# Attention and mixture of experts on one core: queries, keys and values laid out in DRAM by attention steps

## The chip, the core and the metric

The kernel runs on one of the eight cores of a Trainium2 chip. A core has a matrix engine (TensorE, PE in the rows; its weight loads are PEld), VectorE (DVE), ScalarE (ACT), GpSimd (POOL) and SyncE (SP), which here only issues transfers. Sixteen DMA engines move data between DRAM and on-chip memory, which has 128 partitions. The metric is the device time of one execution in microseconds (us); lower is better. Inputs are laid out on the host before the launch, outside of the time.

## What is computed

Attention over 8 batches, 8 heads, 576 positions, with 64 numbers per head. Half of the heads see a window of the last 32 positions, the other half every fourth of the last 128. The result, 4608 rows of 512, goes through a mixture of experts: each row picks one of 4 groups and one of its 4 experts, and is multiplied by that expert's two matrices.

```python
scores = scale * np.matmul(q, k.transpose(0, 1, 3, 2))
mask_plain = (rel >= 0) & (rel < window)
mask_dil = (rel >= 0) & (rel < window * dilation) & (rel % dilation == 0)
...
attn = np.exp(scores)
attn = attn / (np.sum(attn, axis=-1, keepdims=True) + 1e-09)
return np.matmul(attn, v).astype(np.float32)
...
h = np.maximum(xg[mask_e] @ w1[g, e], 0.0)
ye = h @ w2[g, e]
out[tok_idx] = combined[:, None] * ye
```

## The kernel before

Attention comes first, until about 150 us, and the experts after it. Attention is a loop over 36 steps (`for s in range(NT + 3)`, L944). A step takes 64 positions of a pair of batches, for all heads; it is software-pipelined: in turn `s` the loop issues the scores of step `s` (`scores`, L272), the transposes of step `s-1` (L302), the products with the values of step `s-2` (`av`, L314), and turns the finished rows of step `s-3` (L392). The order of PE and DVE is written out by hand, and that of SP and ACT too.

Three steps are a group `g`; there are 12 groups. Queries, keys and values are loaded by groups, by these functions:

- `load_q` (L109, its transfer L110) fills `qb`, 128 partitions of 3 x 512 numbers, 2 KB for each step. There are three such buffers; the third lies in space that later holds weights and is called `wa` in the rows.
- `load_k` (L112, L114) fills `kb` in two halves (`w` = 0 and 1), each of 64 partitions, every other one, with 1536 numbers. There are two such buffers, so the load of group `g+2` waits until the scores of group `g` are done. The first 256 columns are carried over from the group before (`carry_k`, L116).
- `load_v` (L122, L125) fills `vt` in two halves of 64 partitions with 3 x 520 numbers, 2,080 bytes for each step. There are three buffers; the third is also called `wa` in the rows. GpSimd makes a shifted copy, `vs` (`shift_v`, L127).

All of these loads go out on SP, in program order, with the stores of finished rows (`store_x`, L345, L350, L357, in runs of 1 KB) between them, and, late in the loop, with the first weights of the experts (`load_weights`, L641, runs of 4 KB). SP's transfers share eight semaphores (DMAHW0 to DMAHW7 below), so each transfer waits until the one eight places before it has landed.

At the start (L139 to L163) the loads of groups 0 to 2 are issued in one piece; of group 0, the queries of step 0 come alone, and then those of steps 1 and 2; the values likewise. In the loop, `load_k` of group `g+2` goes out at steps `s % 3 == 2` (first half) and the next `s % 3 == 0` (second half), `load_q` at `s % 3 == 0` and `load_v` at `s % 3 == 1`. For the last group, queries are loaded step by step and values in two cuts (L956, L976).

The function `layout` (L1183) lays the inputs out on the host. Queries of a group (`qa`) are [128, 3, 512], so a partition's three steps are one run of 6 KB in DRAM. Keys (`ka`) are [2, 64, 1536], and values (`va`) [128, 3, 8, 65]: 6,144 and 6,240 bytes a run.

Of the kernel before, what the change touches and what calls it, by code (L numbers as in the profile page):

```python
# [17 lines left out]
P = 128  # L18
# [37 lines left out]
def moe_attention_kernel(ctx, tc, q, k, k0, v, cmask, wgate, wpack, out):  # L56
    nc = tc.nc
# [34 lines left out]
    NQ, NK, NPT = 3, 2, 2  # L92
# [3 lines left out]
    qb = [qp.tile([P, 3, 512], F32, name=f"qb{i}") for i in range(NQ - 1)]  # L96
    qb.append(wa32[0][:, 2048 : 2048 + 3 * 512].rearrange("p (j n) -> p j n", j=3))
    VW = 2 * 3 * 8 * 65
    vt = [qp.tile([P, 2, 3, 8, 65], F32, name=f"vt{i}") for i in range(2)]
    vt.append(wa32[1][:, 0:VW].rearrange("p (w j s c) -> p w j s c", w=2, j=3, s=8))  # L100
    vs = [qp.tile([P, 2, 3, 8, 65], F32, name=f"vs{i}") for i in range(2)]
    kb = [qp.tile([P, 2, KW], F32, name=f"kb{i}") for i in range(NK)]
    pt = [qp.tile([P, 4, P], F32, name=f"pt{i}") for i in range(NPT)]
    st, dd, oo = {}, {}, {}
    three = lambda g: g % 3 if g < NG - 1 else 0
# [1 line left out]
    k0t = wa32[0][:, 0 : 2 * (8 * 96 + 32)].rearrange("p (w c) -> p w c", w=2)  # L107

    def load_q(g, j0=0, j1=3):  # L109
        nc.sync.dma_start(qb[three(g)][:, j0:j1], q[g, :, j0:j1])  # L110

    def load_k(g, halves=(0, 1)):  # L112
        for w in halves:
            nc.sync.dma_start(kb[g % NK][w:P:2, w, 256:], k[g, w])  # L114

    def carry_k(g):  # L116
        if g % 3 == 0:
# [4 lines left out]
    def load_v(g, cuts=(0, 3)):  # L122
        for j0, j1 in zip(cuts, cuts[1:]):
            for r in range(2):
                nc.sync.dma_start(vt[three(g)][r:P:2, r, j0:j1], v[g, 64 * r : 64 * r + 64, j0:j1])  # L125

    def shift_v(g, j0=0, j1=3):  # L127
        to, own, last = vs[g % 2], vt[three(g)], vt[three(g - 1)]
# [10 lines left out]
    first = ExitStack()  # L139
    first.enter_context(tc.manual_schedule(engines={mybir.EngineType.SP, mybir.EngineType.Activation}))  # L140
    load_q(0, 0, 1)
    nc.scalar.dma_start(masks[:, 0:2], cm[:, 0:2])
    nc.scalar.activation(warm, id32[:, 0:1], AF.Exp)
# [10 lines left out]
    for w in range(2):  # L154
        nc.sync.dma_start(k0t[w:P:2, w, 0 : 8 * 96], k0[w])
    load_q(0, 1, 3)
    load_k(0)
    load_v(0, (0, 1, 3))
    nc.gpsimd.dma_start(masks[:, 2:], cm[:, 2:])
    load_k(1)  # L160
    load_q(1)
    load_q(2)
    load_v(1)  # L163

    ones = cp.tile([P, P], BF16, name="ones")
# [778 lines left out]
    for s in range(NT + 3):  # L944
# [3 lines left out]
        if s % 3 == 2 and s // 3 + 2 < NT // 3:  # L948
            load_k(s // 3 + 2, (0,))
# [12 lines left out]
        if start:  # L962
            n = start[0]
# [10 lines left out]
        if s % 3 == 1 and 2 <= s // 3 + 2 < NG - 1:  # L974
            load_v(s // 3 + 2)
# [4 lines left out]
        if start:  # L980
            n = start.pop()
# [201 lines left out]
def layout(q, k, v, moe_w_group, moe_w_expert, moe_w1, moe_w2):  # L1183
    import numpy as np

    def seqs(a):
        a = np.asarray(a)
        d = a[:, 4:].reshape(B, 4, CLS, 4, D).transpose(0, 1, 3, 2, 4).reshape(B, 4, S, D)
        return np.stack([a[:, :4], d], axis=1).reshape(NBP, 2, 2, 2, 2, S, D)

    qs, ks, vs = seqs(q), seqs(k), seqs(v)
    qa = qs.reshape(NBP, 2, 2, 2, 2, 3, 3, 2, 32, D)
    qa = qa.transpose(0, 5, 9, 4, 6, 1, 2, 3, 7, 8).reshape(12, P, 3, 512)
    kpad = np.concatenate([np.zeros_like(ks[..., :32, :]), ks], axis=-2).reshape(*ks.shape[:5], 19, 32, D)
    blocks = lambda b: kpad[..., b, :, :].reshape(*ks.shape[:5], len(b) * 32, D)
    kg = [blocks([6 * i + b for b in (2, 4, 6, 1, 3, 5)]).reshape(*ks.shape[:5], 6, 32, D) for i in range(3)]
    ka = np.stack([a.transpose(0, 4, 7, 5, 1, 2, 3, 6) for a in kg], axis=1).reshape(12, 2, 64, 6 * 256)
    k0 = blocks([0, 2, 1])[0].transpose(3, 5, 0, 1, 2, 4).reshape(2, 64, 8 * 96)
    vw = vs.reshape(NBP, 2, 2, 2, 2, 3, 3, 2, 32, D)[..., ::-1, :, :]
    va = vw.transpose(0, 5, 4, 7, 8, 6, 1, 2, 3, 9).reshape(12, P, 3, 8, D)  # L1200
    va = np.concatenate([va, np.full_like(va[..., :1], 1.0 / SX)], axis=-1)

    cmask = np.full((2, 2, 32, len(MASKS), 2, 64), -1e9, np.float32)
    for mi, J in enumerate(MASKS):
        for a in range(2):
            for qq in range(32):
                i = 64 * J + 32 * a + qq
                for kd in range(2):
                    start = 0 if kd == 0 else (i // CLS) * CLS
                    for kk in range(64):  # L1210
                        half = (1 - a) * (kk // 32 - 1) - a * (kk // 32)
                        j = i - qq + 32 * half + kk % 32
                        if 0 <= i - j < 32 and j >= start:
                            cmask[:, a, qq, mi, kd, kk] = 0.0
    cmask = cmask.reshape(P, -1).astype(mybir.dt.np(BF16))
    wg = np.concatenate([np.asarray(moe_w_group), np.asarray(moe_w_expert).transpose(1, 0, 2).reshape(DM, 16)], axis=1)
    wg = np.concatenate([wg, np.zeros((DM, 12), wg.dtype)], axis=1)
    wgate = wg.reshape(4, P, 32).transpose(1, 0, 2).reshape(P, -1)
    w1 = np.asarray(moe_w1).reshape(NE, 4, P, FF).transpose(0, 2, 1, 3).reshape(NE, P, 4 * FF)
    w2 = np.asarray(moe_w2).reshape(NE, 8, P, DM).transpose(0, 2, 1, 3).reshape(NE, P, 8 * DM)  # L1220
    wpack = np.concatenate([w1, w2], axis=2).reshape(NE * P, 8192)
    c = np.ascontiguousarray
    return dict(q=c(qa), k=c(ka), k0=c(k0), v=c(va), cmask=c(cmask), wgate=c(wgate), wpack=c(wpack))
# [21 lines left out]
```

## Time and profile before

| | |
|---|---|
| median of 3 runs | 564.97 us (563.19 to 570.15) |
| the profiled execution's own time | 562.74 us |
| its span, from the first to the last instruction | 561.0 us |
| busy share of the span | PE 95%, PEld 69%, DVE 66%, ACT 57%, POOL 40% |
| packets of the queue that SP issues on (q1) | 72258, 113.65 MB, 65.7% of the 16 DMA engines |
| chain that ended last, by engine | PE 82%, DMA 6%, DVE 5%, issue 2%, ACT 2%, SP 2% |

The chain is followed back from the last instruction, at each step to what released it. A busy PE is not PE at its peak, because matmuls are pipelined and their ends are modelled. The packets of a queue take a share of 16 engines' time; a stretch of 1 us holds 16 us of engine time. "Landing" is the time from a transfer's issue to its semaphore.

### The profile page before, as it was taken

The numbers are of one execution on the slowest core, as the hardware profiler recorded it, in microseconds if no ns is written. First come the engines' busy times: TensorE is split into PE (matmuls) and PEld (weight loads), VectorE is DVE, ScalarE is ACT, GpSimd is POOL, SyncE is SP. The second block draws the span as 40 slices with busy tenths as digits, with TensorE's granted clock in tenths as the row PEclk, the third lists the DMA queues.
The fourth block names the chain that finished last, engine by engine and source line by source line (L and its number), as shares of the span: only waits on it lengthen the run. The fifth ranks groups of instructions, "written<-read, shape, count | busy, mean of one in ns | idle before, by whom it ended". The sixth has DMA issues, their size and how long they took to land.

```text
span 561.0 us, 16459 instructions
## 1 busy us (share of the span) xinstructions
PE 535.4 (95%) x6577; PEld 385.9 (69%) x6577; DVE 370.7 (66%) x846; ACT 317.1 (57%) x563; POOL 223.2 (40%) x211
## 2 busy tenths in 40 slices
PE   6899989997798999999999999999999999999995
PEld 3688878776676676556666666675766756787893
DVE  8776876876777336473868596757657667658650
ACT  6565546575555236464646564656656747647741
POOL 6796665758731423302231614133251421221212
PEclk9999999998999999999999999999999999999999
DMA  8988998798393726958697778779798798897731
GB/s 286 395 285 278 331 275 282 231 315 275 103 316 107 252 68 167 295 162 230 193 292 187 261 193 276 181 249 280 233 302 230 251 327 218 287 327 238 264 103 31
DMA packets 79265, 134.31 MB, mean 239 GB/s; under 512 B 42988, under 2 KB 52630, under 8 KB 79186
## 3 DMA queue, kind: packets, MB, share of 16 engines
q1 hardware_dynamic: 72258, 113.65, 65.7%
q0 software_dynamic: 6784, 19.51, 10.6%
q8 instruction: 53, 0.87, 0.6%
q14 instruction: 26, 0.21, 0.1%
q10 hardware_dynamic: 144, 0.07, 0.0%
HBM read 106.16 MB, written 19.29 MB: 224 GB/s over the span
## 4 chain that ended last, share of the span: by engine, by line
PE 82%; DMA 6%; DVE 5%; issue 2%; ACT 2%; SPq 2%; POOLq 0%; ACTq 0%; DVEq 0%
PE a L748 32%; PE y L841 26%; PE o L314 4%; PE y L859 4%; PE s L272 4%; DMA qb<-q 4%; PE yt L876 3%; PE t L302 3%; DMA kb<-k 2%; PE tx L392 2%; SPq L357 1%; PE lt_ps L417 1%; PE s L253 1%; DMA w<-wpack 1%; DVE wb2l L659 1%
## 5 line engine op out<-in xcount | busy, mean ns | idle before, releaser
L812 POOL DMA_INDIRECT out<-yr,sent x31 | 34.4, 1109 | 220.3 <-ACT yr L811 204.0
L756 DVE SCALAR_TENSOR_TENSOR hl<-a,hh 128x256 f16<-128x256 f32 (+13 forms) x144 | 61.1, 425 | 91.5 <-ACT hh L755 91.3
L748 PE MATMUL a<-xs,wb1h 128*128 128x256 f16 (+7 forms) x576 | 97.8, 275 | 2.5 <-DVE hl L756 2.5
L748 PE MATMUL a<-xs,wa 128*128 128x304 f16 (+7 forms) x864 | 96.6, 272 | 0.0
L755 ACT ACTIVATE hh<-a 128x256 f16<-128x256 f32 (+13 forms) x144 | 55.8, 388 | 63.0 <-PE a L748 62.2
L748 PEld LDWEIGHTS <-wa 128*128 128x128 f16 x864 | 79.2, 98 | 16.4 <-issue 0.2
L841 PEld LDWEIGHTS <-hh 128*128 128x128 f16 x480 | 46.9, 98 | 54.8 <-issue 1.2
L659 DVE SCALAR_TENSOR_TENSOR wa<-w,wa 128x1024 f16<-128x1024 f32 x58 | 69.5, 1217 | 19.1 <-ACT wa L662 19.1
L748 PE MATMUL a<-xs,wb1l 128*128 128x256 f16 (+7 forms) x288 | 78.3, 275 | 0.0
L841 PE MATMUL y<-wa,hh 128*128 128x512 f16 x240 | 73.9, 379 | 0.0
L662 ACT ACTIVATE wa<-w 128x1024 f16<-128x1024 f32 x64 | 66.8, 1055 | 1.5 <-DMA w<-wpack 1.3
L748 PEld LDWEIGHTS <-wb1h 128*128 128x128 f16 x576 | 55.1, 98 | 15.2 <-issue 3.0
L811 ACT ACTIVATE yr<-y,cs 128x512 f32<-128x512 f32 (+3 forms) x31 | 21.3, 687 | 64.4 <-issue 32.1
L687 POOL DMA_INDIRECT xr<-xd,sent x41 | 41.9, 1022 | 29.9 <-DVE sent L675 16.7
L659 DVE SCALAR_TENSOR_TENSOR wb2l<-w,wb2h 128x1024 f16<-128x1024 f32 x32 | 38.3, 1219 | 17.1 <-ACT wb2h L662 17.1
L303 ACT COPY pt<-t 128x512 f32<-128x512 f32 x36 | 21.1, 586 | 44.7 <-PE t L302 44.4
L841 PE MATMUL y<-wb2h,hh 128*128 128x512 f16 x120 | 45.6, 380 | 0.0
L841 PE MATMUL y<-wb2h,hl 128*128 128x512 f16 x120 | 45.5, 379 | 0.0
L841 PE MATMUL y<-wb2l,hh 128*128 128x512 f16 x120 | 45.5, 379 | 0.0
L841 PE MATMUL y<-wa,hl 128*128 128x512 f16 x120 | 45.5, 379 | 0.0
L314 PE MATMUL o<-vs,pt 128*32 128x130 f32 x576 | 40.4, 278 | 3.8 <-POOL wa L657 1.4
L282 DVE TENSOR_REDUCE mx<-s 128x8 f32<-128x512 f32 x36 | 24.6, 685 | 25.0 <-PE s L272 24.8
(206 smaller groups left out, 1073.1 us busy)
## 6 DMA issues: line engine op xcount, KB each, us to landing
w<-wpack SPq DMA_DIRECT2D x128, 512.0 KB, 5.1
kb<-k SPq DMA_DIRECT2D x24, 384.0 KB, 4.6
vt<-v SPq DMA_DIRECT2D x14, 390.0 KB, 7.1
qb<-q SPq DMA_DIRECT2D x7, 768.0 KB, 6.2
xd<-x SPq DMA_DIRECT2D x24, 192.0 KB, 5.8
wa<-v SPq DMA_DIRECT2D x6, 390.0 KB, 7.5
wa<-q SPq DMA_DIRECT2D x3, 768.0 KB, 8.6
xd<-x SPq DMA_DIRECT2D x32, 48.0 KB, 4.4
```

The source lines that it names most:

```text
L272: nc.tensor.matmul(s[32 * j : 32 * j + 32, c].rearrange("p w k -> p (w k)"), qv[:, (sl * 2 + a) * 32 : (sl * 2 + a) * 32 + 32], kv[:, :, f ...
L282: nc.vector.tensor_reduce(mx, s, axis=AX.X, op=ALU.max)
L314: nc.tensor.matmul(o[32 * j : 32 * j + 32, c // 2, at : at + 130], pt[n % NPT][:, c, 32 * j : 32 * j + 32], t[:, :, jl, bb * 4 + c, :], st ...
L659: nc.vector.scalar_tensor_tensor(l, w32, SW, h, ALU.mult, ALU.subtract)
L662: nc.scalar.mul(parts(i)[0], w32s[i], SW)
L687: nc.gpsimd.indirect_dma_start(out=xr[0:n], out_offset=None, in_=xd[0:known, :], in_offset=bass.IndirectOffsetOnAxis(ap=ent[0:n, t : t + 1 ...
L748: nc.tensor.matmul(a[:, 0:cap], ww[:, c * FF + f * P : c * FF + f * P + P], xx[:, c, 0:cap], start=(i == 0), stop=(i == len(mm) - 1),)
L755: nc.scalar.activation(hh[:, f, 0:cap], a[:, 0:cap], AF.Relu)
L756: nc.vector.scalar_tensor_tensor(hl[:, f, 0:cap], a[:, 0:cap], 0.0, hh[:, f, 0:cap], ALU.max, ALU.subtract)
L812: ins = nc.gpsimd.indirect_dma_start(out=out, out_offset=bass.IndirectOffsetOnAxis(ap=ent[0:n, t : t + 1], axis=0), in_=yr[0:n, :], in_off ...
L841: nc.tensor.matmul(yp, h[:, f, t * P : t * P + n], ww[:, f * DM : f * DM + DM], start=(i == 0), stop=(i == len(mm) - 1),)
L859: nc.tensor.matmul(yp[q * (P // g) : q * (P // g) + n, 0:wd], h[:, f, t * P : t * P + n], ww[:, f * DM + q * wd : f * DM + q * wd + wd], s ...
```

## The change

The arrays that the host hands over are transposed: queries of a group become [3, 128, 512], keys [2, 3, 64, 512], values [3, 128, 520]. Each step's part of a load is then one contiguous block. The load itself is a transfer of the same bytes to the same places, whose source has three runs of 2 KB (2,080 bytes for values) per partition where it had one of 6 KB. Loads of two steps of a group have two runs where they had one; loads of one step keep their run of 2 KB and lie closer together.

```diff
     def load_q(g, j0=0, j1=3):
-        nc.sync.dma_start(qb[three(g)][:, j0:j1], q[g, :, j0:j1])
+        nc.sync.dma_start(qb[three(g)][:, j0:j1], q[g, j0:j1].rearrange("j p n -> p j n"))
 
     def load_k(g, halves=(0, 1)):
         for w in halves:
-            nc.sync.dma_start(kb[g % NK][w:P:2, w, 256:], k[g, w])
+            to = kb[g % NK][w:P:2, w, 256:].rearrange("p (i n) -> p i n", i=3)
+            nc.sync.dma_start(to, k[g, w].rearrange("i p n -> p i n"))
...
             for r in range(2):
-                nc.sync.dma_start(vt[three(g)][r:P:2, r, j0:j1], v[g, 64 * r : 64 * r + 64, j0:j1])
+                to = vt[three(g)][r:P:2, r, j0:j1].rearrange("p j s c -> p j (s c)")
+                nc.sync.dma_start(to, v[g, j0:j1, 64 * r : 64 * r + 64].rearrange("j p n -> p j n"))
...
-    qa = qa.transpose(0, 5, 9, 4, 6, 1, 2, 3, 7, 8).reshape(12, P, 3, 512)
+    qa = qa.transpose(0, 5, 9, 4, 6, 1, 2, 3, 7, 8).reshape(12, P, 3, 512).transpose(0, 2, 1, 3)
...
-    ka = np.stack([a.transpose(0, 4, 7, 5, 1, 2, 3, 6) for a in kg], axis=1).reshape(12, 2, 64, 6 * 256)
+    ka = np.stack([a.transpose(0, 4, 7, 5, 1, 2, 3, 6) for a in kg], axis=1).reshape(12, 2, 64, 3, 512)
+    ka = ka.transpose(0, 1, 3, 2, 4)
...
+    va = va.reshape(12, P, 3, 520).transpose(0, 2, 1, 3)
```

The order of instructions is the same on every engine. What SP issues at the start, ahead of the loop, reads so before the change; a row is a transfer, target and source, its shape and the semaphores it waits for:

```order
L125 DMA vt_110<-v 64x1040 [waits DMAHW2_49]
L114 DMA kb_115<-k 64x1536 [waits DMAHW3_49,DVE_49]
L114 DMA kb_115<-k 64x1536 [waits DMAHW4_49,Activation_49]
L110 DMA qb_109<-q 128x1536 [waits DMAHW5_49]
L110 DMA wa_91<-q 128x1536 [waits DMAHW6_49]
L125 DMA vt_111<-v 64x1560 [waits DMAHW7_49,Activation_49]
```

and so after it, at the same place on SP:

```order
L127 DMA vt_110<-v 64x2x520 [waits DMAHW2_49]
L115 DMA kb_115<-k 64x3x512 [waits DMAHW3_49,DVE_49]
L115 DMA kb_115<-k 64x3x512 [waits DMAHW4_49,Activation_49]
L110 DMA qb_109<-q 128x3x512 [waits DMAHW5_49]
L110 DMA wa_91<-q 128x3x512 [waits DMAHW6_49]
L127 DMA vt_111<-v 64x3x520 [waits DMAHW7_49,Activation_49]
```

No row moved and no wait was added or removed; only the shapes differ, and the line numbers of what stands below `load_k`.

## Rows read from the trace of the kernel before

**Rows 1.** Busy time by engine in three stretches, granted clock, DMA share, GB/s

```profile
core 0: us, PE busy (x) PEld busy (x) DVE busy (x) ACT busy (x) POOL busy (x), PEclk, DMA share, GB/s
18.00:111.00 93.00, 90.50 (x2061) 74.95 (x2061) 69.38 (x180) 53.23 (x122) 65.71 (x58) 1.00 0.88 294
111.00:150.00 39.00, 33.29 (x689) 27.61 (x684) 27.51 (x83) 25.72 (x53) 27.76 (x21) 0.96 0.80 252
150.00:561.00 411.00, 400.83 (x3688) 276.82 (x3687) 259.67 (x529) 227.21 (x380) 117.15 (x110) 1.00 0.74 223
```

**Rows 2.** Waits from 18 to 150 us: who waited for what, us, times, longest

```profile
PE s L272 <- DMA kb<-k: 2.3, 1, 2.3
...
PE s L272 <- DMA qb<-q: 1.8, 1, 1.8
...
PEld s L272 <- DMA kb<-k: 0.3, 1, 0.3
```

**Rows 3.** PE's timeline: start, us, what, and the idle time before with its releaser

```profile
18.00 0.43 PE L272 MATMUL s<-kb,qb 128*32 128x128 f32 x8 [1.84 <-DMA qb<-q]
...
129.87 0.38 PE L272 MATMUL s<-kb,qb 128*32 128x128 f32 x5 [2.35 <-DMA kb<-k]
```

**Rows 4.** Busy time by engine in two short stretches, columns as in rows 1

```profile
130.40:133.80 3.40, 3.40 (x57) 3.01 (x49) 1.96 (x5) 0.00 (x0) 3.32 (x3) 0.50 0.95 339
134.00:140.00 6.00, 5.54 (x123) 4.48 (x121) 4.35 (x21) 5.07 (x12) 5.20 (x5) 1.00 0.92 283
```

**Rows 5.** The chain that ended last, in order: start us, us, what

```profile
3.63 6.60 DMA kb<-k
...
10.25 7.62 DMA qb<-q
...
53.07 0.51 SPq L114
...
53.62 5.34 DMA qb<-q
...
58.98 0.69 DVE x L370
...
126.32 3.42 DMA kb<-k
```

**Rows 6.** DMA issues: target, source, count, KB each, median us to landing

```profile
kb<-k SPq DMA_DIRECT2D x24, 384.0 KB, 4.6
vt<-v SPq DMA_DIRECT2D x14, 390.0 KB, 7.1
qb<-q SPq DMA_DIRECT2D x7, 768.0 KB, 6.2
...
wa<-v SPq DMA_DIRECT2D x6, 390.0 KB, 7.5
wa<-q SPq DMA_DIRECT2D x3, 768.0 KB, 8.6
...
vt<-v SPq DMA_DIRECT2D x4, 260.0 KB, 5.8
...
qb<-q SPq DMA_DIRECT2D x1, 512.0 KB
```

**Rows 7.** DMA queues, 12.5 to 15 us and then 1.8 to 3.0 us

```profile
DMA packets 201, 1.05 MB, mean 422 GB/s; under 512 B 29, under 2 KB 29, under 8 KB 201
...
q1 hardware_dynamic: 201, 1.05, 101.2%
...
q1 hardware_dynamic: 91, 0.19, 52.8%
q10 hardware_dynamic: 78, 0.04, 11.6%
```

**Rows 8.** Issues on SP: duration ns min/median/max, first and last start us

```profile
L114 SPq DMA_DIRECT2D kb<-k x24: 472/489/1259, 3.6 to 126.3; - x24
...
L110 SPq DMA_DIRECT2D qb<-q x12: 334/584/1047, 0.8 to 121.5; - x12
...
L345 SPq DMA_DIRECT2D xd<-x x24: 581/637/1487, 24.8 to 158.1; - x24
```

## The prediction

> **What bounds the kernel now.** I began with the three stretches by engine [rows 1]. From 18 to 111 us, the even part of the attention loop, TensorE (PE) is busy 90.50 of 93.00 us while the DMA engines are busy for 0.88 of the time. From 111 to 150 us PE is busy 33.29 of 39.00, at a mean granted clock of 0.96. From 150 us to the end PE is busy 400.83 of 411.00 us, and queries, keys and values are no longer loaded. So PE bounds the kernel nearly everywhere, and a change to these loads can act only where PE waits for one of them.
>
> The list of waits says where that is. After 18 us PE waited for a load of queries once, 1.8 us, and for a load of keys once, 2.3 us, and TensorE's weight load adds 0.3 [rows 2]. The PE timeline gives the places: the first score matmuls of group 1 start at 18.00 after 1.84 us of waiting for `qb<-q`, and those of group 11 (the last) at 129.87 after 2.35 us for `kb<-k` [rows 3]. The second wait costs more than itself: from 130.4 to 133.8 the granted clock is 0.50, that is 1.2 GHz of 2.4, and from 134 on it is 1.00 again [rows 4]. Before the clock fell the engine had done nothing for those 2.35 us. At half rate the 3.4 us did the work of 1.7, so 1.7 us were lost.
>
> The chain that ended last has DMA in the same places [rows 5]: `kb<-k` from 3.63 for 6.60 us and `qb<-q` from 10.25 for 7.62 us at the start, and `kb<-k` from 126.32 for 3.42. It also runs through SP's issues to `qb<-q` at 53.62 and from its landing to `DVE x` at 58.98. There it is nearly a tie, since PE itself is 97% busy in that stretch [rows 1].
>
> **What the change does.** No instruction moves and no byte is added: each load of queries, keys and values keeps its place on SP, its target and its semaphores. Only its runs are cut in three, because the steps of a group now lie apart in DRAM.
>
> How many more runs? A load of 768 KB for `qb` or `wa<-q` (7 + 3 of them) has 128 runs of 6 KB; each of 24 `kb` loads of 384 KB has 64; each of 14 + 6 value loads of 390 KB has 64 [rows 6]. That is 1,280 + 1,536 + 1,280 = 4,096 runs which become three, so 8,192 more. The one query load of 512 KB (128 runs) and the four value loads of 260 KB (64 each) go from one run to two: 384 more. Together **8,576 more runs**. Loads of a single step (256 KB, 130 KB) keep theirs.
>
> What does one more run cost? From 12.5 to 15 us the queues carry almost nothing but 6 KB runs: 201 packets, 29 of them small, 101.2% of 16 engines over 2.5 us [rows 7]. That is 40.48 us of engine time; less 29 small ones at some 10 ns (below), 40.2 / 172 = 234 ns a run. From 1.8 to 3.0 us the mask load on queue 10 shows 78 packets of 512 B and 11.6% of 16 x 1.2 us [rows 7], so 28.6 ns each. A line through both is 0.0365 ns a byte and **9.9 ns a packet**. A 2 KB run should then take 84.6 ns, three of them 254: 20 ns more than one of 6 KB. All of it: 8,576 x 9.9 / 16 = 5.3 us of the 16 engines' time, over 132 us of attention.
>
> The Trainium skill (DMA: Bandwidth & Descriptors, "Why small descriptors are slow") gives about 3 cycles a packet beside one per 32 bytes. By it, as an estimate, three packets instead of one are 6 cycles on 195, or 3.1%, 7 ns where the line gives 20; the whole would be 2.0 us of engine time instead of 5.3. The rows decide, and I keep 9.9 ns.
>
> **Issue.** SP's time for one issue, median, is 0.489 us for a key load (64 runs), 0.584 for a query load (128), and 0.637 for the store of L345, which has 64x3 runs [rows 8]. A key load will have the shape of that store, so I take 0.64, **+0.15 us**. For a query load of 384 runs I have bounds: 0.64 if the shape alone counts, and 1.27 if time goes with runs (0.637 / 192 x 384).
>
> **The sum, place by place.**
> *Start.* Before group 1's queries land, the engines work through what was issued ahead: one query load to two runs (128 more), both key halves of group 0 (256), values of group 0 (128), both key halves of group 1 (256) and these queries (256): 1,024 x 9.9 / 16 = **0.6 us**. The engines are full there [rows 7], so nothing hides it; PE would start at 18.6. Bounds: 0.2 (half of these runs moving while SP still issues) and 2.3, for a wait of 1.84 + 0.63 = 2.5 us is as long as the one after which the clock fell; the same 1.7 us could be lost here.
> *18 to 111 us.* PE waits for no load in this stretch, so the 768 runs more of a group, 768 x 9.9 / 16 = 0.5 us of engine time, are hidden by PE's work; if that cover were gone they would cost those 0.5 us a group. I take **0.3 us**, for two longer key issues (53.07 and the one before it) in the chain ahead of 53.62. Bounds 0 (the tie falls to PE) and 0.9 (two value issues at the same 0.15 and a query issue at 0.3 on the path too).
> *111 to 150 us.* Two key halves lie between 113.9 and 129.7: 256 x 9.9 / 16 = 0.16, and two issues, 0.30: **0.5 us** more in the wait of 2.35. Bounds 0 and 1.0 (the low clock lasting longer).
> *After 150 us.* Nothing of these loads is left: 0.
> Sum: **+1.4 us**. The profiled execution took 562.74 us (its span is 561.0), so 564.1. The median of the three runs shown is 564.97, which gives 566.4; between the two I forecast **565.3 us**.
>
> **Rivals.**
> *The DMA engines become the bound* (12%). Were attention paced by them, all 5.3 us would be on the path: 568 to 570 us. For it speaks their share of 0.88; against it, that PE is 97% busy in the same stretch and waits for none of them [rows 1, 2].
> *The clock falls at the start too* (13%). As above, +1.7: 566 to 568 us. It shows as a granted clock of 0.50 soon after 18 us.
> *Slower by over 2%: a 2 KB run costs far more than the line says* (8%). The kernel's very first load has 2 KB runs; queue 1 shows 91 packets and 52.8% of 16 x 1.2 us [rows 7], 111 ns each. At that price three runs are 333 ns, 99 more than now; 4,288 runs of 6 KB' worth of that, over 16, is 26.5 us of engine time. Attention leaves the engines idle for 132 - (0.88 x 93 + 0.80 x 39) = 19 us [rows 1], so at least 7.5 us would go on the path, and 512 x 99 / 16 = 3.2 at the start: 574 us, and up to 590 if the idle parts can't be filled because stores wait for compute. It decides from 19 x 16 / 4,288 = 71 ns per three runs, or 102 ns a run. Against it: that load ran into empty, just started queues, and the 512 B runs beside it took only 28.6 ns.
> The Trainium skill (Perfetto Trace Analysis, "DMA Optimizations") says that going from 2 KB to 4 or 8 KB can raise the throughput dramatically, which speaks against this change. It gives no price, and the steady 6 KB row and the 512 B row do not agree with a dramatic loss at 2 KB.
> *No cost, or a gain* (5%). If runs of 2 KB are stopped less by the stores between them, keys of group 11 could land earlier. The whole wait and its low clock are 2.35 + 1.7 = 4.0 us: 559 to 563 us. No row here shows a shorter run being held up less.
>
> **How the numbers follow.** The likeliest case (62%) covers 562 to 568 us with the spread of the runs shown. I let the range reach from 561.5 to 571: that takes in the first two rivals and most of the gain, and leaves out the slow rival and some of the tails. About 2% is 11 us here and is what can be told from no change. Only the slow rival exceeds it upward (0.08); for a gain over 2% there is too little waiting to be had (0.02); the rest, 0.90, is within.
>
> **What would show it.** Queue 1 should carry some 8,600 more packets. The first scores of group 1 should start near 18.6 us and those of group 11 wait some 2.8 us. A key issue should take 0.64 us. From 18 to 111 us PE should still be some 97% busy with no new wait for a load. I am wrong if PE waits for queries or keys in the middle of the loop, if steady 2 KB runs take over 100 ns, or if a clock of 0.50 shows in a new place.

## The result, and the profile after

The changed kernel takes **566.91 us** (median of 22 runs, 562.41 to 570.67). The kernel before, run beside it on the same chip, takes 564.0 (22 runs, 560.29 to 570.15). The ratio is **1.0054, with a 95% interval of 1.003 to 1.0078**: 3.0 us slower (1.7 to 4.4). The forecast was 565.3 us, in a range of 561.5 to 571.0, made of +1.4 us. So the time lies in the range and the change is within 2%, but the loss is about twice the sum, and the interval leaves +1.4 just outside.

The profiled execution of the changed kernel took 568.52 us with a span of 566.7. It stands 5.7 us above the span of before, more than the medians differ. The pair of traces therefore tells where time can go, not how much goes there on average. Line numbers below `load_k` are higher by one or two than before.

The three stretches, as in [rows 1]:

```profile
18.00:111.00 93.00, 89.07 (x1979) 73.62 (x1982) 68.09 (x175) 50.90 (x116) 61.55 (x54) 0.98 0.89 288
111.00:150.00 39.00, 31.06 (x672) 25.96 (x665) 26.81 (x80) 23.85 (x50) 29.25 (x22) 0.96 0.86 263
150.00:561.00 411.00, 405.94 (x3784) 281.00 (x3784) 262.52 (x535) 229.92 (x388) 120.44 (x111) 1.00 0.75 223
```

The last stretch is fuller only because the end moved from 561.0 to 566.7. In the first two, TensorE (PE) does less in the same time (matmuls 2061 to 1979, 689 to 672), and the DMA engines' share rises, most from 111 to 150 us: 0.80 to 0.86. The list of waits from 18 to 150 us says for what:

```profile
POOL vs L132 <- DMA vt<-v: 12.7, 5, 5.0
POOL vs L132 <- DMA wa<-v: 8.0, 2, 4.7
...
PE s L274 <- DMA kb<-k: 4.9, 3, 3.4
...
PEld s L274 <- DMA kb<-k: 2.6, 3, 1.6
...
PE s L274 <- DMA qb<-q: 1.8, 1, 1.8
```

PE and its weight load now wait for keys six times, 4.9 and 2.6 us, against 2.3 and 0.3 [rows 2]. The wait for queries is what it was. GpSimd's shifted copy `vs` waits 20.7 us for values, where the same two rows of before have 5.4 and 2.1.

Part of the keys' waiting is new in place. From 18 to 111 us alone the kernel before has one wait for keys, the 0.3 us of the weight load in [rows 2]. The changed kernel shows there:

```profile
PEld s L274 <- DMA kb<-k: 1.9, 2, 1.6
...
PE s L274 <- DMA kb<-k: 1.2, 1, 1.2
```

PE's timeline, to be laid beside [rows 3]: the transposes in turn 2, the first scores of group 1 (step 3) and of step 4, and the first scores of the last group (step 33):

```profile
15.27 0.66 PE L304 MATMUL t<-id,d 128*128 128x128 f32 x4 [0.63 <-ACT d L297]
...
17.92 1.55 PE L274 MATMUL s<-kb,qb 128*32 128x128 f32 x32 [1.78 <-DMA qb<-q]
...
22.67 0.54 PE L274 MATMUL s<-kb,qb 128*32 128x128 f32 x12
...
135.19 1.94 PE L274 MATMUL s<-kb,qb 128*32 128x128 f32 x32 [3.38 <-DMA kb<-k]
```

And two short windows behind those two waits, columns as in [rows 1] and [rows 4], with the first window of the kernel before as the third line:

```profile
18.20:21.70 3.50, 3.50 (x66) 3.11 (x56) 1.77 (x5) 0.00 (x0) 0.53 (x1) 0.53 1.05 386
134.40:137.90 3.50, 2.71 (x52) 2.74 (x56) 0.69 (x1) 0.00 (x0) 3.33 (x3) 0.51 1.03 373
...
18.20:21.70 3.50, 3.50 (x93) 2.98 (x89) 2.35 (x5) 1.05 (x3) 0.68 (x2) 1.00 1.05 416
```

The queries of group 1 land no later than before (scores at 17.92, before at 18.00). But the granted clock is 0.53 behind that wait, near 1.2 GHz of 2.4, where before it stayed at 1.00. Behind the last group's wait it is low in both kernels, and the wait itself has grown from 2.35 to 3.38 us.

With the start of each step's first score matmul in both traces, the 5.7 us can be laid out in order:

| stretch | before, us | after, us | difference |
|---|---|---|---|
| start to step 3 | 18.00 | 17.92 | -0.1 |
| steps 3 to 4 (clock 0.53) | 3.14 | 4.75 | +1.6 |
| steps 4 to 31 | 99.47 | 101.34 | +1.9 |
| steps 31 to 34 (last group) | 14.71 | 16.28 | +1.6 |
| step 34 to the end | 425.68 | 426.41 | +0.7 |

These are differences of two single executions. The traces of the experiments show how far the same stretches move by themselves. From step 4 to 31, two kernels whose loop loads are as before take 101.0 us (start3) and 103.7 (kf1), and four with runs of 2 KB take 100.6 to 102.1 (busy3, loop3, pad3, kf3). From step 34 on, where none of these loads is left, the same six take 426.6 to 432.9 us. So the pair alone doesn't show what the change costs in these stretches.

The DMA side shows what the change did to the transfers: queue 1 over the whole span, the same queue from 12.5 to 15 us, and the issues on SP, as in [rows 7] and [rows 8].

```profile
q1 hardware_dynamic: 80834, 113.65, 66.1%
```

```profile
DMA packets 515, 1.00 MB, mean 398 GB/s; under 512 B 29, under 2 KB 29, under 8 KB 515
...
q1 hardware_dynamic: 515, 1.00, 105.0%
```

```profile
L115 SPq DMA_DIRECT2D kb<-k x24: 602/612/2012, 3.6 to 129.5; - x24
...
L110 SPq DMA_DIRECT2D qb<-q x12: 372/593/1377, 0.8 to 126.2; - x12
```

80,834 less 72,258 is 8,576 packets. In the short window 105.0% of 16 x 2.5 us is 42.0 us; less 29 small ones at some 10 ns, 41.7 / 486 = **85.8 ns a run of 2 KB**, where 84.6 was forecast. The traces also have each packet by itself. From 0 to 150 us the median is 234 ns for 6,144 bytes (before), 84 for 2,048 (the change), 46 for 1,024 (all6) and 27 for 512 (q12). That is a straight line with 8 to 9 ns a packet on top of the bytes, and three runs of 2 KB take 18 ns more than one of 6 KB. A key issue takes 0.612 us and a query issue 0.593 in the median; four of those twelve query loads are of one step, and whole groups in the loop take 0.60 where before they took 0.58.

### The profile page after: what moved, and what is told of

Its sections match the earlier page's. It is cut to its first block, busy times and chain, and to the rows that moved or that the text cites. A ratio compares the mean times of both kernels' runs of the same rounds, so it can differ in the third digit from the quotient of the medians.

```text
span 566.7 us, 16459 instructions
## 1 busy us (share of the span) xinstructions
PE 536.8 (95%) x6577; PEld 387.2 (68%) x6577; DVE 371.6 (66%) x846; ACT 316.3 (56%) x563; POOL 225.2 (40%) x211
## 3 DMA queue, kind: packets, MB, share of 16 engines
q1 hardware_dynamic: 80834, 113.65, 66.1%
## 5 line engine op out<-in xcount | busy, mean ns | idle before, releaser
L814 POOL DMA_INDIRECT out<-yr,sent x31 | 36.0, 1163 | 218.8 <-ACT yr L813 202.7
L661 DVE SCALAR_TENSOR_TENSOR wa<-w,wa 128x1024 f16<-128x1024 f32 x58 | 69.6, 1216 | 20.5 <-ACT wa L664 20.5
```

The lines of the kernel that those rows point to most:

```text
L661: nc.vector.scalar_tensor_tensor(l, w32, SW, h, ALU.mult, ALU.subtract)
L814: ins = nc.gpsimd.indirect_dma_start(out=out, out_offset=bass.IndirectOffsetOnAxis(ap=ent[0:n, t : t + 1], axis=0), in_=yr[0:n, :], in_off ...
```

## The experiments

Each run is compared with the kernel before on the same chip in the same session. That kernel's median went from 564.0 to 569.1 us between sessions, so ratios count, not times. The change itself was measured in a session of its own. k12, v12, all12 and kf12 rest on three or four executions each. Most kernels load through a helper that takes a group's array as `n` blocks in DRAM, with one table to choose `n` for queries, keys and values. `n = 1` is the layout before, 3 that of the change (2 KB), 6 gives runs of 1 KB and 12 of 512 B (520 for values). Targets, bytes and the places of the loads on SP stay.

| run | layout | ratio (95%) | us |
|---|---|---|---|
| the change | all in 2 KB | 1.0054 (1.003 to 1.0078) | +3.0 |
| q12 | queries in 512 B | 1.0026 (0.9986 to 1.0066) | +1.5 |
| k12 | keys in 512 B | 1.0133 (1.006 to 1.0206) | +7.6 |
| v12 | values in 520 B | 1.0151 (1.0081 to 1.0222) | +8.6 |
| all12 | all in 512 B | 1.0415 (1.036 to 1.0469) | +23.6 |
| start3 | groups 0 to 2 in 2 KB | 0.9998 (0.996 to 1.0037) | -0.1 |
| loop3 | groups 3 to 11 in 2 KB | 1.0019 (0.9976 to 1.0062) | +1.1 |
| pad3 | 2 KB runs in the old place | 1.0039 (1.0002 to 1.0076) | +2.2 |
| busy3 | change, PE kept busy at the start | 1.0035 (1.0001 to 1.007) | +2.0 |
| all6 | all in 1 KB | 1.0111 (1.0055 to 1.0167) | +6.3 |
| kf12 | all12, keys issued earlier | 1.0353 (1.0277 to 1.043) | +19.9 |
| kf3 | change, keys issued earlier | 1.0006 (0.997 to 1.0043) | +0.3 |
| kf1 | before, keys issued earlier | 1.0001 (0.9971 to 1.0031) | 0.0 |

### Which loads cost: q12, k12, v12, all12

```diff
+PIECES = dict(q=lambda g: 12, k=lambda g: 1, v=lambda g: 1)
```

This is q12; k12 and v12 have the 12 at keys or values, and all12 has it at all three. The dose is made larger so that one array's part can be told from none. Each of the three adds nearly the same number of packets.

> Queries alone in runs of 512 B (12 for each 6 KB), keys and values in 6 KB runs as before. That is 16,512 more packets, at 9.9 ns 10.2 us of the 16 engines' time. Theory A (one queue: only the added engine time counts, whichever array it comes from): +2 to +6 us, and the same within 2 us as with keys or values cut. Rival B (keys, which have two buffers only, are the load that comes late): +1.5 us at most. Rival C (only the clock's fall at the start matters): +1 to +2 us, a granted clock of 0.50 just after the first scores of group 1, no wait for keys in the middle of the loop.

> Keys alone in runs of 512 B, queries and values in 6 KB runs. 16,896 more packets, 10.5 us of engine time. Theory A: +2 to +6 us, as with queries or values. Rival B: +5 us or more, and PE's waits for keys in the middle of the loop add up to 4 us or more. Rival C: +1 to +2 us, all of it at the start.

> Values alone in runs of 520 B, queries and keys in 6 KB runs. 16,640 more packets, 10.3 us of engine time. Theory A: +2 to +6 us, as with queries or keys. Rival B: +1.5 us at most. Rival C: +1 to +2 us, all of it at the start.

> Queries, keys and values all in runs of 512 B (520 for values): 50,048 more packets, 31 us of engine time, where the engines were idle for 19 of 132 us of attention. Theory A: the engines become the bound, +12 us at least and up to +31; the DMA share from 18 to 111 us goes to 0.97 or more. Rival B: the effect of the keys alone, within 2 us. Rival C: +2 to +3 us.

Measured: +1.5 (-0.8 to +3.8), +7.6 (3.4 to 11.7), +8.6 (4.6 to 12.6) and +23.6 us (20.5 to 26.7). Queue 1 carried 88,770, 89,154 and 88,898 packets, so at 9.9 ns a packet the added engine time is 10.2 to 10.5 us in each of the first three. It is not the engine time alone that counts: queries cost less than values, beyond the error; against keys the two intervals just touch. Nor is it the keys' own length alone: with keys untouched, v12 costs as much as k12, and it is the *keys* for which PE then waits. The waits of v12 from 18 to 150 us:

```profile
POOL vs L143 <- DMA vt<-v: 16.8, 4, 7.1
...
POOL vs L143 <- DMA wa<-v: 10.0, 2, 5.0
...
PE s L285 <- DMA kb<-k: 7.2, 5, 4.4
...
PEld s L285 <- DMA kb<-k: 4.0, 5, 1.9
```

In k12, whose keys are cut, PE waits for keys no longer than before, where 4 us or more had been expected:

```profile
PE s L285 <- DMA kb<-k: 2.6, 1, 2.6
```

So this trace does not show where k12 loses its 7.6 us. It is of k12's shortest execution, 570.93 us where the median is 575.28.

SP's own waits in v12 show one way in which late values can hold up what follows:

```profile
SPq L370 <- DMA vt<-v: 4.7, 6, 1.4
```

L370 is the store that is L357 before. It stands on SP between the loads and waits for the landing of values issued before it, as the eight semaphores have it: 4.7 us here, where the same row of before has 1.4. It is not shown that this is what makes the keys late: the row has 3.4 us in q12 and 2.8 in k12, whose waits for keys are as before, and all12 has no such row.

With all three the waits for keys are 29.1 us until 150 us, the last group's 7.4 us come after that, and PE is busy 78.84 of 93 us (all12, waits from 18 to 150 us and the first stretch):

```profile
PE s L285 <- DMA kb<-k: 14.7, 6, 4.6
...
PEld s L285 <- DMA kb<-k: 14.4, 5, 5.0
```

```profile
18.00:111.00 93.00, 78.84 (x1667) 65.89 (x1667) 56.38 (x137) 44.15 (x100) 54.06 (x48) 0.93 0.94 246
```

The DMA engines' share of 0.94 stays below the 0.97 that theory A expected. The three single results add up to 17.7 us, less than 23.6, but with an error of some 6 us on the sum and 3 on all12 that does not show that more is lost together.

Why queries cost least was only argued. In the code they are issued up to six steps ahead of their use and have three buffers. A half of the keys is issued three or four steps ahead, and values must be there for the shifted copy two steps after their issue.

### Start or loop: start3 and loop3

```diff
+st = lambda g: 3 if g < 3 else 1
+PIECES = dict(q=st, k=st, v=st)
```

This is start3; loop3 has `1 if g < 3 else 3`.

> Groups 0 to 2 by steps in 2 KB runs as after the change, groups 3 to 11 in 6 KB runs as before it. Theory D (the change costs at two kinds of place: at the start, by the 0.6 us of more packets and by the clock that falls after that wait, 1.7 us; and in the loop and at its end, by keys that land late): +1 to +2 us over the kernel before, granted clock 0.50 for 3.4 us right after the first scores of group 1. Rival E (all of it is the start): +2.5 to +3.5 us. Rival F (all of it is the loop): 0 to +0.6 us.

> Groups 0 to 2 in 6 KB runs as before, groups 3 to 11 by steps in 2 KB runs as after. Theory D: +1 to +2 us over the kernel before; the start as before the change (first scores of group 1 at 18.0, no low clock there), PE's waits for keys after 18 us 4 us or more in total where the kernel before had 2.3. Rival E: 0 to +0.5 us. Rival F: +2.5 to +3.5 us.

Measured: -0.1 us (-2.3 to +2.1) and +1.1 us (-1.4 to +3.5). A cost of the start is not seen in start3, but an interval this wide excludes only one above 2.1 us. In its profile the first scores of group 1 start at 18.12 after a wait of 1.48 us, and no low clock follows, where theory D expected one. The last group, whose loads are as before in start3, waits longer for keys than in the changed kernel:

```profile
133.70 1.23 PE L285 MATMUL s<-kb,qb 128*32 128x128 f32 x32 [3.56 <-DMA kb<-k]
```

In loop3 that wait is 0.65 us, with runs of 2 KB. But keys are late in the loop as in the change, by less, 3.4 us where 4 or more had been expected (18 to 150 us):

```profile
PEld s L285 <- DMA kb<-k: 1.8, 2, 1.4
PE s L285 <- DMA kb<-k: 1.6, 2, 1.0
```

The two halves add up to +1.0 us where the whole has +3.0; with errors of 2 us on each half that is no contradiction.

### Number of runs or their place: pad3

```diff
-        nc.sync.dma_start(qb[three(g)][:, j0:j1], q[g, j0:j1].rearrange("j p n -> p j n"))
+        nc.sync.dma_start(qb[three(g)][:, j0:j1], q[g, :, j0:j1, 0:512])
...
+    gap = lambda a: np.concatenate([a, np.zeros_like(a[..., :16])], axis=-1)
+    qa, ka, va = gap(qa), gap(ka.reshape(12, 2, 64, 3, 512)), gap(va.reshape(12, P, 3, 520))
```

The steps of a partition stay next to each other in DRAM as before. Each is followed by 64 unused bytes, so that three runs cannot become one.

> The rows lie where they lay before the change, a partition's three steps after each other, but with 64 unused bytes after each step, so that each load is made of three runs of 2 KB without being laid out by steps. If the number of runs is what costs: as the changed kernel, +2 to +4 us over the kernel before. If it is the new place of the steps in DRAM (blocks of 128 or 256 KB apart): 0 to +1 us.

Measured: +2.2 us (0.1 to 4.3), with the same 80,834 packets. That is within the +2 to +4 expected of the number of runs, though the interval does not exclude the 0 to +1 of the other theory. From 18 to 150 us it waits like the change (in one of its longest executions, 575.18 us where the median is 570.64):

```profile
POOL vs L132 <- DMA vt<-v: 16.5, 6, 7.9
...
PE s L274 <- DMA kb<-k: 6.2, 4, 4.0
```

So the cut alone is enough to bring the same waits. That blocks now lie 128 to 260 KB apart adds nothing that can be measured here.

### The clock at the start: busy3

```diff
+        if n == 3:
+            keep_busy(8)
```

This is the change, with idle matmuls ahead of the scores of step 3, so that PE is not idle while it waits for queries.

> The changed kernel with 8 idle matmuls (into a buffer that nothing reads) ahead of the first scores of group 1, so that PE works while it waits for those queries. Theory D: the clock does not fall there, steps 3 to 6 take 3.14 us each, and 1.7 us come back in the executions where it fell: 1 to 2 us faster than the changed kernel, +1 to +2 over the kernel before. Rivals that don't need the clock: as the changed kernel, +2.5 to +3.5 us.

Measured: +2.0 us (0.1 to 4.0). The same window as above, in busy3:

```profile
18.20:21.70 3.50, 3.50 (x77) 2.74 (x75) 1.52 (x4) 0.19 (x1) 0.81 (x2) 1.00 1.06 386
```

The clock stays at 1.00 and steps 3 to 4 take 3.14 us again. But the added matmuls ran until 18.9, so the scores started at 18.86 instead of 17.92. That gives back 0.9 of the 1.6 us, so a gain of 0.7 is left, and the time cannot be told from that of the change. The profiled executions show a low clock soon after group 1's wait in the change, pad3, all6, all12 and kf12, and none in start3, loop3, busy3, q12, k12, v12, kf1 and kf3. The loads ahead of step 3 are cut in start3 and kf3 too, so the cut does not always bring it.

The mean granted clock of every execution says how much it is on average, as an estimate. It is 0.9936 over the 22 of the changed kernel, and 0.9947 to 0.9954 over those of the kernel before in four other sessions. Of some 566 us that is 0.6 to 1.0 us more lost to the low clock, at whatever place. In busy3 it is 0.9968 and in pad3, of the same session and with as many packets, 0.9936: 1.8 us of clock won, of which the medians, 570.18 and 570.64, show 0.5.

### A dose between: all6

```diff
+PIECES = dict(q=lambda g: 6, k=lambda g: 6, v=lambda g: 6)
```

> Queries, keys and values all in runs of 1 KB (1,040 B for values): 22,400 more packets than before the change, 13.9 us of the 16 engines' time at 9.9 ns, between the changed kernel (5.3 us, +3.0) and the one in runs of 512 B (31 us, +23.6). If the cost goes with the added engine time from the first packet on (0.57 of it at 2 KB, 0.76 at 512 B): +8 to +11 us. If the engines' idle 19 us have to be used up first and it costs only from there: +2 to +5 us.

Measured: +6.3 us (3.1 to 9.5), between the two expectations, and the interval reaches into both. Queue 1 carried 94,658 packets, 22,400 more than before.

| | change | all6 | all12 |
|---|---|---|---|
| packets added | 8,576 | 22,400 | 50,048 |
| engine time added (estimate, 9.9 ns / 16), us | 5.3 | 13.9 | 31.0 |
| measured, us | 3.0 | 6.3 | 23.6 |
| share of it | 0.57 | 0.45 | 0.76 |

About half of the added engine time arrives at the end for the two smaller doses (their intervals allow 0.2 to 0.8). The engine time is worked out from packets. Queue 1's own share times the span, 368.6 us before, scatters too much to check it at these doses: it is +6.0 us in the change, +0.9 in busy3 and +8.1 in pad3 with as many packets, +6.6 in all6 and +30.1 in all12. From 13.9 to 31.0 us, 17.3 of 17.1 us arrive. The prediction worked out 19 us of idle engine time in attention; the second step of the dose runs beyond that.

### The keys issued earlier: kf12, kf3, kf1

```diff
-            load_k(s // 3 + 2, (0,))
-        if s % 3 == 0 and 2 <= s // 3 + 1 < NT // 3:
-            load_k(s // 3 + 1, (1,))
+            load_k(s // 3 + 2)
```

Both halves go out at `s % 3 == 2`, the second one now ahead of the stores that stood between them on SP. Some of GpSimd's instructions trade places too, so more than the loads differs from the kernel before; kf1 and kf3 have the same order. If late keys are what costs time, this should give it back.

> Queries, keys and values all in runs of 512 B, and the second half of each key load issued on SP right behind the first half, ahead of the four or five stores that stood between them. Theory G (what costs is keys that land late because they stand in SP's queue behind stores and values, each of which waits for the transfer eight places before it): at least 8 of the 23.6 us come back, +8 to +15 us over the kernel before, and PE's waits for keys from 18 us on, 14.7 us on PE and 14.4 on its weight load, fall to less than half. Rival A (the DMA engines' time is the bound, in whatever order): no more than 3 us come back, +20 to +25.

> The changed kernel with the second half of each key load issued right behind the first, ahead of the stores. Theory G: the waits for keys from 18 us on (4.9 us on PE, 2.6 on its weight load) fall below 2 us together, the one of the last group at some 130 us and its low clock are gone; 2 to 5 us faster than the changed kernel, 0 to -2 us against the kernel before. Rival A: as the changed kernel, +2 to +4 us.

> The kernel before with the second half of each key load issued right behind the first, ahead of the stores. Theory G: the wait of 2.35 us of the last group and its low clock (1.7 us) go, so -2 to -4 us, and with runs of 6 KB it is the fastest of all, 1 to 2 us ahead of the same with 2 KB runs. Rival A: 0 to -1 us.

**kf12**: +19.9 us (15.6 to 24.3) where all12 has +23.6. The waits for keys fall from 29.1 to 2.2 us, but others come up (18 to 150 us, then the first stretch):

```profile
DVE x L383 <- DMA xd<-x: 10.5, 6, 3.6
PE o L327 <- DVE x L383: 9.1, 8, 1.8
...
PE s L285 <- DMA qb<-q: 4.4, 1, 4.4
...
PE s L285 <- DMA kb<-k: 2.2, 2, 1.2
```

```profile
18.00:111.00 93.00, 82.97 (x1816) 68.98 (x1816) 59.29 (x147) 46.28 (x105) 54.68 (x49) 0.96 0.97 265
```

With the keys out of the way the stores `xd<-x` are late, and VectorE waits for the buffers that they free. The engines' share is 0.97. At this dose the engines are the bound, and the order on SP mostly decides which transfer is late. The waits for keys fell as theory G expected, but only 3.7 us came back where it expected 8 or more; the time is nearly the +20 of rival A.

**kf3**: +0.3 us (-1.7 to +2.4) against before, where the change has +3.0 (1.7 to 4.4). PE waits for no keys after 18 us. Steps 32 and 33 follow each other at 3.14 us without a wait or a low clock, and the first stretch stays near [rows 1]:

```profile
127.08 1.08 PE L285 MATMUL s<-kb,qb 128*32 128x128 f32 x32
...
130.22 1.08 PE L285 MATMUL s<-kb,qb 128*32 128x128 f32 x32
```

```profile
18.00:111.00 93.00, 88.61 (x1992) 72.55 (x1987) 68.06 (x176) 52.11 (x119) 62.68 (x56) 1.00 0.91 292
```

Against the kernel before, the cost of the change is gone within the error. The two intervals still overlap, so 2.7 us is what the middle values say, not a proof. The closer partner is kf1, of the same session, which differs from kf3 only in the layout. There the medians are 565.05 and 564.2 us and the means 565.0 and 563.8, so +0.8 to +1.2 us, with an error of about as much. So with keys issued earlier some of the cost may be left. Nor is the low clock gone: kf3's trace has 0.51 at 155.9 us instead, and its twelve executions have a mean of 0.9944, where those of the kernel before have 0.9952.

**kf1**, the same edit without the change: 0.0 us (-1.6 to +1.8), where 2 to 4 us had been expected from the last group's wait of 2.35 us and its low clock. Its profile shows no wait at step 33, but from the scores of step 10 to those of step 11 it took 6.28 us, with an idle PE for 1.93 us and a clock of 0.50 from 43.9 us on. So a wait and a low clock can come elsewhere; why they did was not settled. Its runs lie closer together (12 runs, 561.74 to 565.16) than those of before (19 runs, 560.52 to 568.36). No version was measurably faster than the kernel before.

## Why the prediction was right, and where it was short

**What held.** PE paces the kernel and the loss stays within 2%. The price of a packet held (85.8 ns a 2 KB run against 84.6), and so did the count, 8,576. A key issue takes 0.612 us where 0.64 was taken. A query issue takes 0.593 (0.60 for whole groups), below the lower of its two bounds: its time does not go with the number of runs.

**Its own signs.** Of the three signs of being wrong that it named, two came: PE waits for keys in the middle of the loop, and a clock near 0.5 shows in a new place. PE is busy 95.8% from 18 to 111 us, where 97% was expected. That the time is in the range owes much to the range's width of 9.5 us, which took in two rivals and the spread of the runs. The +1.4 us are half of what was measured.

**Rivals.** *A 2 KB run costs far more* decided from 102 ns a run; it took 85.8. The first load's 111 ns a packet [rows 7] did not come back in the steady loop. *No cost, or a gain* is refuted by an interval that begins at +1.7. *The DMA engines become the bound* is not so at 2 KB, since 0.57 of the estimated engine time arrives; it is so at 512 B (kf12). *The clock falls at the start too* happened in the profiled execution, at +1.6 us where 1.7 was worked out; start3 and busy3 give it no share that can be measured in time, and by the mean clocks it is 0.6 to 1.0 us at all places together.

**The start (+0.6).** It rested on the engines being full until group 1's queries land. The trace has them land at the same time, and start3 shows -0.1. Larger doses do move that start, to 18.99 us in all6 and 20.27 in all12, about half of the 1.8 and 4.2 us that the same count of packets gives. So the term was too large, unless the clock falls.

**18 to 111 us (+0.3): the step that failed.** It said that PE waits for no load in this stretch, so that more engine time is hidden by PE's work. A wait of zero says nothing of how much slack a load has, and it was not quite zero: 0.3 us of [rows 2], PE's weight load for keys, lie in this stretch. Here keys, and values above all, had little slack. The landing of values (390 KB) goes from 7.1 to 8.3 us and of queries from 6.2 to 7.2 [rows 6]; keys are then waited for, 1.2 and 1.9 us in this stretch. The other traces repeat it:

| loads from group 3 on | PE's and its weight load's waits for keys, 18 to 111 us | wait of the last group |
|---|---|---|
| as before: the kernel before, start3 | 0.3, 0 | 2.35, 3.56 |
| only queries in 512 B: q12 | 1.0 | 1.40 |
| only keys in 512 B: k12 | 0 | 2.60 |
| only values in 520 B: v12 | 6.4 | 4.40 |
| all in 2 KB: the change, pad3, loop3, busy3 | 3.1, 3.5, 2.8, 0.4 | 3.38, 3.98, 0.65, 1.85 |
| all in 1 KB: all6 | 4.0 | 1.16 |
| all in 512 B: all12 | 19.4 | 7.42 |

With values cut, keys are late in the middle of the loop, but for busy3; with values in runs of 6 KB they hardly are. That v12 makes PE wait for untouched keys shows that a load is held up by its neighbours; by which path is not shown. The prediction costed each load for itself. How much of the +3.0 us comes from here is open, since the length of this stretch scatters by more.

**111 to 150 us (+0.5).** In the pair of traces the last wait went from 2.35 to 3.38 us, +1.0, the upper bound, and from step 31 to 34 it is +1.6. From the issue of the last key half to the scores it is now 135.19 - 129.5 = 5.7 us, before 129.87 - 126.3 = 3.6. But in the table above this wait does not go with the length of the runs, but for the largest dose: it is 3.56 us in start3 and 0.65 in loop3. So the runs show neither this term nor its mechanism; that one pair of traces comes near it is luck.

**The rule on small descriptors.** By 3 cycles a packet, as the Trainium skill has it (DMA: Bandwidth & Descriptors, "Why small descriptors are slow"), three runs cost 7 ns more than one. The trace has 3 x 85.8 - 234 = 23 ns by the window, and 18 ns by the medians of the packets. The measurement decides: 4.8 us of engine time by the medians, nearer the 5.3 of the line than the 1.9 that the rule gives here (the prediction has 2.0). What the prediction took from the Trainium skill (Perfetto Trace Analysis, "DMA Optimizations") is said there of batching small transfers into larger ones. Here every transfer kept its size and only its runs were cut, so these runs do not test it.

What stays open is how the +3.0 us divide between the middle of the loop, the last group and the clock. Single profiles differ in this, and the parts are as small as the error. That late keys in the loop carry a part of it is what v12, the table and kf3 together make likely; it is not shown how large a part.

## What to carry to other kernels

Price a cut in runs by packets first: here 8 to 10 ns each, over 16 engines. Then ask not whether PE is busy, but how much slack each load has between its issue and its first use, and what stands in the same queue: with engines at a share of 0.88, about half of the added engine time, as worked out from packets, reached the end though nearly every load looked hidden. A load with little slack can be issued ahead of stores in its queue; that took all or most of the waits for keys away at both doses, but at the larger one another transfer became the late one. And read such small losses from more than one trace: the last group's wait moved from 0.65 to 3.98 us between traces with the same runs.

## What the runs showed of the hardware

- **The same wait, another clock.** Before, PE was idle for 1.84 us ahead of the scores of group 1, and 0.20 us shortly before, and the granted clock stayed at 1.00. In the changed kernel it was idle for 1.78 us, and 0.63 us shortly before, and the granted clock fell to 0.53; the next step took 4.75 us instead of 3.14. The length of the single wait did not tell whether it would cost its double.
- **Issue time hardly follows the number of runs.** On SP a query load of a whole group took 0.60 us with 384 runs where it took 0.58 with 128. A key load went from 0.489 to 0.612 us with 64 and 192 runs.
- **Where runs lie did not show.** Runs of 2 KB next to each other (pad3, 1.0039) and 128 to 260 KB apart (the change, 1.0054) cannot be told apart.
- **A packet has a fixed price.** The median packet took 27 ns for 512 bytes, 46 for 1,024, 84 for 2,048, 159 for 4,096 (the experts' weights) and 234 for 6,144. That is one line, with 8 to 9 ns a packet.
